# Attention, MoE and routed MoE on one core: inputs laid out for long rows, one VectorE step less per 64-bit piece, and a new order up to the first expert

## The chip, the cores and the metric

One core of one Trainium2 chip runs the whole program. The metric is device time in microseconds from launch to end. Three runs of the kernel before took 1063.85, 1066.41 and 1070.76 us; the median is 1066.41 us. In what follows PE is TensorE with its weight loads (PEld), DVE is VectorE, ACT is ScalarE, POOL is GpSimd, and SP is SyncE, whose queue issues nearly all DMAs. Every engine takes its own instructions strictly in the order in which they were written.

## The reference, cut to what matters

Three layers follow each other. Attention has 4 batches, 8 heads, 576 positions and head size 64, and sums two parts: a coarse attention over q, k and v averaged over groups of 4 positions, and a local one in which a position sees its 3 neighbours on each side. Then come a dense MoE layer with a squared relu, and a layer of 8 experts of which each token uses the two with the highest noisy gate value.

```
q_d, k_d, v_d = mean over groups of 4 positions
out = repeat(softmax(q_d k_d^T / 8) v_d, 4) + softmax(mask(q k^T / 8, |i-j| < 4)) v
x   = out as (2304, 512)
x   = relu(x @ w_in)^2 @ w_out                  # w_in (512, 2048), w_out (2048, 512)
y   = x @ w_gate + log1p(exp(x @ w_noise)) * noise;  top 2 of 8, softmax weights
out[token] += weight * (relu(x @ w1[e]) @ w2[e])  # for its two experts
```

w_in and w_out are float64 and reach the chip as 64-bit words, whose two halves the kernel joins to a float32 itself; everything else is float32.

## The kernel before, in words

Attention works on units: one batch, one pair of heads, one of two parts of the positions, so 32 units, numbered u = 8*batch + 4*part + pair. The dense layer works on 9 chunks of 256 tokens; a chunk's first product has 8 steps (M, 24 matmuls each), whose results are squared and split into a high and a low f16 half (r), and the second product has 8 steps (Y). All products are of split f16 operands, so three matmuls stand for one. The expert layer keeps an expert's weights split in the same way.

What sets the order is a table of names, ORDER, written out by hand up to the first expert's products: the program calls one small function per name, and each function's instructions go to the ends of their engines' queues. Names that the text uses:

- qk, vw, vg: DMA loads of q and k, of the windows of v for the local part, and of v in groups of 4.
- TQ, TK (L263 to L277): the transposes of q and k on PE, three blocks of 96 rows at a time into PSUM, and the copy of each half to qT or kT.
- GQ, GK (L279 to L289): sums of q and k over groups of 4, for batch 0 on POOL (three adds), for the others on DVE (one reduction).
- S, D (L307, L321): local and coarse scores. PT: transposes of the weights. PV, PW: products with v (L429 to L440). xa, xb: sums and f16 halves of the chunk's x.
- il, ib, ic, ij, is, in: one of 8 pieces of w_in: load; bits (two DVE steps, L528 and L529); scale (ACT, L533); join (DVE, L540); squares (ACT); column norms (PE). wS is the scale of all of w_in, whose maximum over partitions is made by POOL (L1003); wh, wl are the f16 halves (L1010, L1017).
- ol, oB, oc, oj, os, of, oh, oo: the same for 8 pieces of w_out, which hold a quarter of the columns and half of the rows each; oh and oo are the halves (L1073, L1078).
- yh, yl: steps of the second product of chunk 0, by quarters of the columns, as w_out arrives (L671). Y8 is the first full step of chunk 1 (L647).

A piece of 1 MB sits in a raw buffer (4 of them). For w_out the joined values go to one of four other places, and the raw buffer is free after the squares. q and k of batch 0 lie in the buffer of w_in's high half or in one buffer "qk"; a load into a buffer waits on SP's queue until its last reader is done, and all later loads wait behind it.

Two landmarks serve as stage bounds: M0, the first matmul of the dense layer (L608), and Y8.

Of the kernel before, what the change touches and what calls it, by code (L numbers as in the profile page):

```python
# [20 lines left out]
NP = H // 2  # L21
# [31 lines left out]
qk0 TQ0 TKa0 qk1 TQa1 GK0 GQ0 TK1 GQ1 il0 ib0 qk2 S0 ic0 D0 GK1 md0 S1 ed0 ml0 el0 il1 ij0 nl0 TQ2 is0 TKa2 qr0  # L53
nd0 GQ2 ib1 ic1 D1 md1 ed1 ml1 GK2 TR0 el1 nl1 nd1 PT0 S2 D2 GR0 md2 vg0 vm0 il2 ml2 el2 vs0 PT1 qk3 TQa3 ib2
ic2 TKa3 il3 ed2 S3 nl2 ij1 vw0 PV0 vg2 GQ3 GK3 D3 ib3 is1 vg1 nd2 ij2 ic3 ij3 vm1 vs1 vm2 ml3 vs2 el3 md3 il4
ib4 xa0 PT2 nl3 S4 D4 md4 vg3 vm3 Xa0 ml4 ed3 nd3 qr1 TRa1 S5 in1 is2 Xb0 in2 GR1 ic4 il5 ib5 vw1 PV1 el4 nl4
ij4 xb0 vs3 il6 is3 qr2 ic5 ij5 is4 ib6 ed4 xa1 PT3 D5 md5 il7 nd4 ic6 ij6 in4 ed5 ib7 TRa2 S6 xb1 ml5 is6 vw2
PV2 ic7 ij7 in3 in6 is5 xa2 in5 in0 el5 is7 PT4 ol0 oB0 vw3 in7 wS0 PV3 ol1 xb2 qr3 whd2 oc0 oj0 GR2 D6 oB1 xa3
wh0 wl0 wh7 TRa3 S7 wh3 xb3 wh1 os0 ol2 oB2 GR3 ol3 ol4 D7 wl1 wl2 oc1 oj1 wh5 M0 oB3 oc2 oj2 vw4 ra0 M1 M2 os1
ol5 oc3 wl7 vw5 os2 oj3 wl3 ra1 wl5 os3 of3 ol6 wh6 wl6 wh4 wl4 PW4 ob0 ra2 ol7 oh3 oh2 oB6 M3 M4 yh8 yh9 yh10  # L60
oo3 oB7 ra3 M5 oo2 oc6 oc7 oj7 oj6 ra4 yl8 yh11 os7 yl9 yl10 yl11 oB5 yh12 os6 of7 of1 nl5 ra5 M6 nd5 oh7 oo7
oh6 oh1 oc5 yl12 oh0 oo6 M7 oo1 oB4 PT5 oo0 yl24 yh24 yh13 oc4 yh25 yh0 oj4 yl25 qk4 TQa4 yh1 yl13 oj5 TKa4 yl26
xbd4 yl0 yh26 yl1 yh2 os4 md6 os5 yl2 SD0 pz0 ml6 yh27 yh3 of5 yl27 yl3 vg4 yh4 ra6 ed6 md7 vw6 yh28 el6 PW5
yh29 oh5 GK4 qk5 oh4 yl28 S8 TQa5 ed7 yl29 yh5 GQ4 D8 yh16 TKa5 pf5 yh17 nl6 nd6 yl4 PT6 ml7 el7 S9 vm4 pf3 xbd5
# [24 lines left out]
md30 D31 Y45 ra49 vw29 vw30 M50 el30 gf9 PT29 rd50 M51 ge9 gg9 ml31 ra51 PW29 xbd29 Y46 ed30 M52 nl30 nd30 el31
nl31 r52 Y47 ga10 md31 ed31 ga11 M53 r53 nd31 PT30 M54 PW30 gb10 xbd30 ra54 Y48 PT31 Y49 gb11 vw31 PW31 xbd31  # L90
gc10 gd10 gf10 M55 rd55 Y50 M56 AD0 gc11 gd11 Y51 M57 r56 r57 le0 pe0 pe1 ge10 gg10 pe2 pe3 pe4 gf11 Y52 M58 r58
Y53 M59 ge11 Y54 gg11 r59 M60 rd60 pe5 pe6 Y55 ga12 ga13 gb12 gb13 M61 r61 M62 pe7 Y56 gc12 gd12 Y57 gc13 pe8
ra62 gf12 Y58 gd13 gf13 Y59 M63 ge12 gg12 Y60 M64 Y61 pe9 r63 pe10 ge13 r64 pe11 gg13 M65 r65 pe12 pe13 Y62 M66
r66 Y63 ga14 ga15 gb14 gc14 M67 r67 M68 pe14 r68 Y64 Y65 gd14 Z0 M69 gb15 Z1 gf14 Y66 gc15 gd15 Z2 ge14 M70 gg14
ra69 M71 gf15 Z3 ge15 gg15 Y67 Y68 Y69 pe15 Z4 r70 Y70 Z5 pe16 r71 Y71 ga16 lr0 gb16 Z6 Z7 ga17 gb17 cm2 cm3 cm1
gc16 gd16 gf16 le1 cm0 cm6 cm7 cm5 ge16 gg16 gc17 cm4 pe17 gd17 pe18 pe19 pe20 gf17 pe21 pe22 pe23 cw0 ge17 gg17
cw1 pe24 pe25 pe26 lr1 cw2 cm9 cm11 pe27 cm10 cm8 pe28 cm15 cm14 lr2 cm13 cm12 pe29 pe30 cw4 pe31 pe32 cw3 pe33
le2
"""


@with_exitstack
def moe_kernel(ctx, tc, q, k, v, w_in, w_out, w_gate, w_noise, noise, w1, w2, out):
# [175 lines left out]
    def att_gi(b, hp, i, h=None):  # L279
# [6 lines left out]
        else:  # L286
            nc.gpsimd.tensor_tensor(dd, d4[:, :, 0], d4[:, :, 1], op=OP.add)
            for r in (2, 3):
                nc.gpsimd.tensor_tensor(dd, dd, d4[:, :, r], op=OP.add)  # L289
# [1011 lines left out]
```

## Time and profile before

| what | us |
|---|---|
| median of three runs | 1066.41 |
| span of the profiled execution | 1059.6 |
| median minus span | 6.8 |
| PE busy in the span | 945.8 (89%) |
| DVE busy | 623.7 (59%) |
| ACT busy | 485.3 (46%) |
| POOL busy | 161.9 (15%) |
| M0 starts (timeline) | 94.80 |
| Y8 starts (timeline) | 238.55 |

The page gives the span of the profiled execution, from its first to its last instruction, and not that execution's run time; what lies around the span is taken as the difference to the median. Busy shares over the whole span mix stages: PE has idle time until about 250 us and nearly none from there to 600 us. A DMA count on the page: 170115 packets, of them 129048 under 512 B.

### The profile page before, as it was taken

To read this page: it belongs to the slowest core of one execution; us is meant where nothing else is said; L and a number is where in the kernel's file an instruction comes from. 1 tells how busy PE (TensorE), PEld (TensorE's weight loads), DVE (VectorE), ACT (ScalarE), POOL (GpSimd) and SP (SyncE) were. 2 spreads that over 40 slices of the span, in tenths; PEclk is the share of its full clock that TensorE was granted. 3 is DMA by queue.
4 is the path that set the end of the run, shared out by engine and by line. 5 is a ranking of instruction groups with operands and counts; after the bars stand their busy time and mean duration, and the time that the engine had idled before them with its cause. 6 is when DMAs were issued, how large, how long until landed. Compare 5 with 4: busy or idle time off the path is not lost. (4 is left out here: it accounts for less than half of the span.)

```text
span 1059.6 us, 20935 instructions
## 1 busy us (share of the span) xinstructions
PE 945.8 (89%) x8351; PEld 636.9 (60%) x8351; DVE 623.7 (59%) x1883; ACT 485.3 (46%) x1065; POOL 161.9 (15%) x240
## 2 busy tenths in 40 slices
PE   3545788879999999999999999799999999999994
PEld 2334687655767677677766556465656565656562
DVE  4877896647877777777668674362525252525220
ACT  3656685544625464435445354372717171713110
POOL 5720020000101000100002212102020202021111
PEclk9999898989999999999999999899999999999997
DMA  6672376774223331211511265872737372730212
GB/s 191 187 233 78 121 198 200 215 235 87 82 57 86 74 83 32 61 51 37 191 41 51 68 203 118 234 212 39 217 40 218 40 215 42 217 40 11 39 17 36
DMA packets 170115, 121.69 MB, mean 115 GB/s; under 512 B 129048, under 2 KB 141848, under 8 KB 168984
## 3 DMA queue, kind: packets, MB, share of 16 engines
q1 hardware_dynamic: 161496, 100.52, 33.7%
q0 software_dynamic: 8512, 19.74, 9.3%
q8 instruction: 68, 1.11, 0.4%
q14 instruction: 39, 0.32, 0.1%
HBM read 70.28 MB, written 35.28 MB: 100 GB/s over the span
## 5 line engine op out<-in xcount | busy, mean ns | idle before, releaser
L608 PE MATMUL ph<-x,wih 128*128 128x256 f16 x1152 | 195.5, 275 | 0.0
L901 PEld LDWEIGHTS <-we 128*128 128x128 f16 x1536 | 151.8, 99 | 69.2 <-issue 15.6
L915 PE MATMUL po<-we,h 128*128 128x512 f16 (+1 forms) x840 | 182.4, 379 | 0.0
L608 PE MATMUL ph<-x,wil 128*128 128x256 f16 x576 | 158.4, 275 | 0.0
L901 PE MATMUL phc<-xT,we 128*128 128x384 f16 (+1 forms) x1152 | 154.4, 296 | 3.9 <-DVE h L904 3.9
L915 PEld LDWEIGHTS <-h 128*128 128x128 f16 (+1 forms) x840 | 87.5, 104 | 92.4
L647 PE MATMUL y<-wo,gh 128*128 128x512 f16 x448 | 134.7, 383 | 0.0
L903 ACT ACTIVATE h<-phc 128x384 f16<-128x384 f32 (+1 forms) x112 | 47.5, 430 | 177.1 <-PE phc L901 160.4
L608 PEld LDWEIGHTS <-wih 128*128 128x128 f16 x1152 | 111.4, 99 | 18.8 <-issue 1.0
L917 DVE TENSOR_SCALAR ob<-po,om 128x512 f32<-128x512 f32 (+1 forms) x35 | 26.3, 750 | 146.6 <-PE po L915 146.6
L918 POOL DMA_INDIRECT out_dram<-ob,tk x35 | 53.9, 1539 | 320.0 <-DVE ob L917 174.4
L808 POOL DMA_INDIRECT xs<-row,si x36 | 39.1, 1087 | 320.9 <-DVE xt L456 57.6
L647 PE MATMUL y<-wo,gl 128*128 128x512 f16 x224 | 85.4, 381 | 0.0
L904 DVE SCALAR_TENSOR_TENSOR h<-phc,h 128x384 f16<-128x384 f32 (+1 forms) x112 | 51.8, 476 | 52.0 <-ACT h L903 51.3
L647 PEld LDWEIGHTS <-gh 128*128 128x128 f16 x448 | 41.7, 98 | 42.3 <-issue 2.4
L608 PEld LDWEIGHTS <-wil 128*128 128x128 f16 x576 | 56.9, 99 | 7.1
L616 ACT ACTIVATE r<-ph 128x512 f32<-128x512 f32 x67 | 39.6, 591 | 26.4 <-PE ph L608 18.0
L620 ACT ACTIVATE g<-r 128x512 f32<-128x512 f32 x72 | 45.4, 630 | 11.9 <-DVE r L618 9.8
L630 DVE TENSOR_TENSOR gl<-g,gh 128x512 f16<-128x512 f32 x64 | 44.2, 691 | 9.2 <-ACT gh L629 8.0
L854 DVE SCALAR_TENSOR_TENSOR we<-w1raw,sce,we 128x1024 f16<-128x1024 f32 x32 | 40.5, 1278 | 3.9 <-ACT we L853 3.6
L321 PE MATMUL S<-kT,qT 64*64 64x144 f32 x192 | 22.3, 346 | 21.7 <-POOL qT L289 16.0
L854 DVE SCALAR_TENSOR_TENSOR we<-w2raw,sce,we 128x1024 f16<-128x1024 f32 x32 | 40.7, 1274 | 0.0
(347 smaller groups left out, 1477.3 us busy)
## 6 DMA issues: line engine op xcount, KB each, us to landing
w1raw<-in_moe_w_dram SPq DMA_DIRECT2D x8, 2048.0 KB
w2raw<-in_moe_w_dram SPq DMA_DIRECT2D x8, 2048.0 KB
xs<-zrow SPq DMA_DIRECT2D x8, 1290.0 KB
raw<-in_moe_w_out_dram SPq DMA_DIRECT2D x8, 1024.0 KB
raw<-in_moe_w_in_dram SPq DMA_DIRECT2D x7, 1024.0 KB
out_dram<-zrow SPq DMA_DIRECT2D x1, 4864.0 KB
qk<-in_k_dram SPq DMA_DIRECT2D x28, 144.0 KB
vw<-in_v_dram SPq DMA_DIRECT2D x94, 38.0 KB
```

The lines of the kernel that those rows point to most:

```text
L608: nc.tensor.matmul(ph[:, f], a[:, kk, fo], bb[:, kk], start=(n == 0), stop=(n == 11))
L616: nc.scalar.activation(r, ph, AF.Relu, scale=KAPPA)
L620: nc.scalar.activation(g, r, AF.Square)
L630: nc.vector.tensor_tensor(gl, g, gh, op=OP.subtract)
L647: nc.tensor.matmul(py[c, tt], a[:, o], bb[:, ft], start=(ft == 0 and n == 0), stop=(ft == 15 and n == 2))
L808: st = nc.gpsimd.indirect_dma_start(out=xs, out_offset=bass.IndirectOffsetOnAxis(ap=si[:, kk:kk + 1], axis=0), in_=roww, in_offset=None)
L854: nc.vector.scalar_tensor_tensor(wl[:, o], raws[i][:, o], ss[i], wh[:, o], op0=OP.mult, op1=OP.subtract)
L901: nc.tensor.matmul(ph[:, :n], a[:, fo], xT[:, bb], start=(i == 0), stop=(i == 11))
L903: nc.scalar.activation(hh[:, f], ph[:, :n], AF.Relu)
L904: nc.vector.scalar_tensor_tensor(hl[:, f], ph[:, :n], 0.0, hh[:, f], op0=OP.max, op1=OP.subtract)
L915: nc.tensor.matmul(po, a[:, f, jo], bb[:, do], start=(i == 0), stop=(i == 23))
L918: nc.gpsimd.indirect_dma_start(out=out, out_offset=bass.IndirectOffsetOnAxis(ap=tk[:m], axis=0), in_=ob[:m], in_offset=None, compute_op=OP ...
```

## The change

The host lays five inputs out anew (no arithmetic, only positions). q and k come already transposed, head pair by head pair, one row of 2 x 579 float32 per partition with three zeros behind each: one load of 593 KB takes the place of four to six of 72 to 144 KB, and TQ, TK and their copies are gone. v comes twice, once as windows with the 3 neighbours built in (38 rows of 2 or 3 KB, two copies per unit where there were four), once as groups of 4. w_out comes in the 8 pieces, with rows of 8 KB where they were 1 KB. The sums of q and k (G) are one DVE reduction per head pair, in batch 0 too.

Of a 64-bit piece the low word is now made by ACT (a new step, ia and oa, L495 of the new file), and DVE has one step (L499) where it had two. w_out's joined values stay in the raw buffer, which is free only after the low half oo. The loads of w_in's pieces 4 to 7 go to four places that are unused then. In chunks 1 to 5 the squared halves of the first three steps lie in three more buffers. The order table up to the first expert is new; r replaces its variants ra and rd (the f16 copy is on DVE in all 72 steps), and xb replaces xbd (the high half is on ACT for all 32 units).

```diff
@@ ORDER = """
-qk0 TQ0 TKa0 qk1 TQa1 GK0 GQ0 TK1 GQ1 il0 ib0 qk2 S0 ic0 D0 GK1 md0 S1 ed0 ml0 el0 il1 ij0 nl0 TQ2 is0 TKa2 qr0
+qk0 il0 ia0 vg1 G0 vg0 S0 vm1 ml0 el0 D0 md0 ed0 vm0 ib0 nl0 ic0 qk1 S1 nd0 vg3 vm3 qk2 G1 vs0 ml1 D1 PT0 S2 il1
...
-    def load_qk(b, hp, at_=None):
...
+    def load_qk(b, hp):
+        t = ap.tile([P, 2 * SD + 2 * (S + 3)], F32, tag="qkT", name=f"qkT{b}_{hp}", bufs=4)
+        nc.sync.dma_start(t[:, 2 * SD:], qk_in[b, hp])
+        qk[b, hp] = t
...
-            for j in range(2):
...
-                w = bass.AP(src.tensor, src.offset + (32 * (t0 + i0) - 3) * D, [[D, KW], [32 * D, i1 - i0], [1, D]])
-                nc.sync.dma_start(vt[h0:h0 + KW, i0:i1, j], w)
+            nc.sync.dma_start(vt[h0:h0 + KW, :n].rearrange("k t j d -> k (t j d)"),
+                              vwin[b, hp, :, t0:t0 + n].rearrange("k t c -> k (t c)"))
...
-    def att_ti(b, hp, i, evs=(EV, EV), gs=(0, 1)):
...
-                nc.tensor.transpose(pt[:, r * QT:(r + 1) * QT], src[:, 3 * g + r, :], idf[:QT, :QT])
-            evs[g](dst[:, 288 * g:288 * g + 288], pt[:, :288])
...
+    def att_g(b, hp, eng=None):
+        t = qk[b, hp]
+        dd = t[:, :2 * SD].rearrange("c (w g) -> c w g", w=2)
+        d4 = t[:, 2 * SD:].rearrange("c (w x) -> c w x", w=2)[:, :, :S].rearrange("c w (g r) -> c w g r", r=4)
+        if eng is None:
+            nc.vector.tensor_reduce(dd, d4, AX.X, OP.add)
...
+    xall = wp.tile([P, XB, 2, NP, CH], F16, name="xall")
+    xb = [xall[:, i] for i in range(XB)]
...
+        def low():
+            t_ = st["raw"][:, :, 0]
+            nc.scalar.activation(t_, t_.bitcast(U32), AF.Relu, scale=2.0 ** -29, bias=lob)
+
         def bits():
-            r16 = st["raw"].rearrange("p n w -> p (n w)").bitcast(U16).rearrange("p (n w) -> p n w", w=4)
-            nc.vector.tensor_scalar(r16[:, :, 0], r16[:, :, 1], 13, None, op0=OP.logical_shift_right)
-            nc.vector.tensor_scalar(r16[:, :, 1], r16[:, :, 3], 0x8000, None, op0=OP.bitwise_and)
+            t_, c_ = st["raw"][:, :, 0], st["raw"][:, :, 1]
+            nc.vector.scalar_tensor_tensor(t_, c_, -2 ** 31, t_, op0=OP.bitwise_and, op1=OP.bitwise_or)
...
+        return [load, low, bits, scale, join, st]
...
+        if 0 < c < 6 and fp < GX:
+            gh = ap.tile([P, 512], F16, tag="gh", name="gh", bufs=GX)
+            gl = ap.tile([P, 512], F16, tag="gl", name="gl", bufs=GX)
...
-        def place(h):
...
+            load, low, bits, conv, join, st_ = load_f(None, w_out[h])
...
+            w = (W["in"][1].rearrange("p k f -> p (k f)").bitcast(I32)[:, 2048 * n:2048 * n + 2048] if n < 2 else
+                 xall[:, 2 * n - 3:2 * n - 1].rearrange("p i a k c -> p (i a k c)").bitcast(I32))
...
+def _laid_out(inputs):
+    q, k, v = (np.asarray(inputs[n]) for n in "qkv")
+    qk = np.zeros((B, NP, 2, D, 2, S + 3), q.dtype)
+    for i, a in enumerate((q, k)):
+        qk[..., i, :S] = a.reshape(B, NP, 2, S, D).transpose(0, 1, 2, 4, 3)
...
```

How the change moves instructions, at three places. On PE just ahead of M0 the order before was this (S is a tile of scores, kT and qT transposed k and q, wih and x the dense layer's operands):

```order
L321 MATMUL S<-kT_2_313,qT_2_312 64x144 x4
L276 MATMUL ptq<-idf,qk_3_431 128x96 x3
L307 MATMUL S<-kT_3_437,qT_3_436 32x38 x20
L321 MATMUL S<-kT_3_437,qT_3_436 64x144 x4
L608 LDWEIGHTS wih
L608 MATMUL ph<-x_158,wih 128x256
```
and in the change:

```order
L966 LDWEIGHTS xall
L966 MATMUL pn<-onesb,xall 128x1
L263 MATMUL S<-qkT_0_685 32x38 x16
L577 LDWEIGHTS wih
L577 MATMUL ph<-xall,wih 128x256
```
The transpose and the coarse scores of two units (L321) stood ahead of M0; in the change only column norms and local scores (L263) that need no sum of q or k.

On DVE, pieces of w_in being joined (raw and wil hold raw words, vi the joined values). Before:

```order
L528 TENSOR_SCALAR raw<-raw 128x1024
L529 TENSOR_SCALAR raw<-raw 128x1024
L358 TENSOR_REDUCE rs<-pm_143 128x5
L540 SCALAR_TENSOR_TENSOR vi<-raw 128x1024
L479 SCALAR_TENSOR_TENSOR x_158<-xt,sx_645,x_158 128x256
L540 SCALAR_TENSOR_TENSOR vi<-raw 128x1024
L528 TENSOR_SCALAR wil<-wil 128x1024
L529 TENSOR_SCALAR wil<-wil 128x1024
L456 TENSOR_TENSOR xt<-px,od 128x256
```
and in the change:

```order
L508 SCALAR_TENSOR_TENSOR vi<-raw 128x1024
L499 SCALAR_TENSOR_TENSOR raw<-raw 128x1024
L436 SCALAR_TENSOR_TENSOR xall<-xt,sx_456,xall 128x256
L314 TENSOR_REDUCE rs<-pm_143 128x5
L499 SCALAR_TENSOR_TENSOR wil<-wil 128x1024
L319 TENSOR_SCALAR rs<-rs 128x5
L320 RECIPROCAL rs<-rs 128x5
L508 SCALAR_TENSOR_TENSOR vi<-raw 128x1024
L413 TENSOR_TENSOR xt<-px,od 128x256
```
Two steps per piece and one join (L528, L529, L540) have become one step and one join (L499, L508), with the attention's small steps between them as before.

On SP, the loads of w_in from the fifth on, before:

```order
L524 DMA raw<-in_moe_w_in_dram 128x2048
L194 DMA wil<-in_v_dram 72x4x256
L227 DMA wih<-in_q_dram 96x3x64 x2
L524 DMA raw<-in_moe_w_in_dram 128x2048
L259 DMA vw_152<-in_v_dram 38x4x64 x4
L524 DMA wil<-in_moe_w_in_dram 128x2048
L227 DMA wih<-in_q_dram 96x3x64 x2
L524 DMA raw<-in_moe_w_in_dram 128x2048
```
and in the change, from the second on (four loads of q and k with two of v are partly ahead of it):

```order
L491 DMA raw<-in_moe_w_in_dram 128x2048
L190 DMA wih<-in_vgrp_dram 72x1024
L223 DMA qkT_3_337<-in_qk_dram 128x1158
L491 DMA raw<-in_moe_w_in_dram 128x2048
L230 DMA vw_151<-in_vwin_dram 38x512 x2
L491 DMA raw<-in_moe_w_in_dram 128x2048
L491 DMA wil<-in_moe_w_in_dram 128x2048 x2
L230 DMA vw_152<-in_vwin_dram 38x512 x2
L491 DMA xall<-in_moe_w_in_dram 128x2048
L230 DMA vw_151<-in_vwin_dram 38x512 x2
L491 DMA xall<-in_moe_w_in_dram 128x2048
```
The loads of a second half of q into buffers still read by transposes (L227) stood between w_in's; now q and k of batch 0 have four buffers of their own and stand ahead, and only window loads (L230) are between.

## Rows read from the trace of the kernel before

**Rows 1.** Windows to M0, to Y8, beyond; per engine busy us (instructions).
```profile
core 0: us, PE busy (x) PEld busy (x) DVE busy (x) ACT busy (x) POOL busy (x), PEclk, DMA share, GB/s
0.00:94.80 94.80, 39.12 (x568) 28.41 (x568) 61.14 (x104) 46.59 (x100) 45.70 (x89) 1.00 0.61 178
94.80:238.50 143.70, 116.09 (x1611) 100.23 (x1609) 105.96 (x238) 90.27 (x216) 7.46 (x27) 0.89 0.65 189
238.50:600.00 361.50, 360.98 (x3573) 248.25 (x3570) 272.79 (x1119) 171.19 (x440) 37.38 (x73) 1.00 0.26 71
```

**Rows 2.** PE's waits before M0: us in total, times, longest.
```profile
PE S L321 <- POOL qT L289: 16.0, 4, 10.0
PE ptp L384 <- POOL pm L366: 11.6, 2, 11.0
```

**Rows 3.** Timeline, four engines: start us, us, engine, work [idle before <-releaser].
```profile
12.80 1.31 DVE L528 TENSOR_SCALAR raw<-raw 128x1024 uint16<-128x1024 uint16 x1
...
65.50 0.43 POOL L366 TENSOR_TENSOR pm<-pm,rs 128x152 f32<-128x152 f32 x1 [9.68 <-issue]
...
81.01 0.38 POOL L1003 PARTITION_ALL_REDUCE n2w<-cm__866  x1 [8.05 <-issue]
...
86.66 1.27 DVE L1017 SCALAR_TENSOR_TENSOR wil<-vi,s_in,wih 128x1024 f16<-128x1024 f32 x1
...
88.71 0.30 POOL L287 TENSOR_TENSOR qT<-qT 128x72 f32<-128x72 f32 x1 [7.33 <-issue]
...
89.96 1.23 PE L321 MATMUL S<-kT,qT 64*64 64x144 f32 x8 [10.01 <-POOL qT L289]
...
94.80 0.61 PE L608 MATMUL ph<-x,wih 128*128 128x256 f16 x2
```

**Rows 4.** The same windows, the transposes alone (L276).
```profile
94.80:238.50 143.70, 8.82 (x72) 6.97 (x72) 0.89 0.65 189
238.50:600.00 361.50, 7.98 (x72) 7.14 (x72) 1.00 0.26 71
```

**Rows 5.** Groups on DVE, 0 to 262 us: xcount, busy us, mean ns.
```profile
L529 DVE TENSOR_SCALAR raw<-raw 128x1024 uint16<-128x1024 uint16 x15 | 21.9, 1459 | 0.5
L528 DVE TENSOR_SCALAR raw<-raw 128x1024 uint16<-128x1024 uint16 x15 | 20.5, 1364 | 3.7 <-DMA raw<-in_moe_w_out_dram 3.7
...
L540 DVE SCALAR_TENSOR_TENSOR vi<-raw 128x1024 int32<-128x1024 int32 x7 | 9.3, 1336 | 0.0
...
L285 DVE TENSOR_REDUCE qT<-qT 128x144 f32<-128x576 f32 x6 | 4.4, 743 | 0.0
```

**Rows 6.** Groups on ACT, 0 to 262 us.
```profile
L533 ACT ACTIVATE raw<-raw 128x1024 f32<-128x1024 f32 x15 | 17.3, 1151 | 19.6 <-DVE raw L529 19.5
...
L277 ACT COPY qT<-ptq 128x288 f32<-128x288 f32 x20 | 7.4, 395 | 19.2 <-PE ptq L276 19.1
```

**Rows 7.** Timeline of SP's DMA issues.
```profile
38.06 12.71 SPq L259 DMA_DIRECT2D vw<-in_v_dram  x4
50.88 0.99 SPq L524 DMA_DIRECT2D wil<-in_moe_w_in_dram  x1
...
71.96 24.25 SPq L522 DMA_DIRECT2D raw<-in_moe_w_out_dram  x3
...
216.06 17.60 SPq L259 DMA_DIRECT2D vw<-in_v_dram  x4
```

**Rows 8.** PE's waits from M0 to Y8.
```profile
PE px L437 <- DMA vw<-in_v_dram: 10.9, 6, 5.4
PE y L671 <- DVE wo L1078: 5.1, 1, 5.1
PE pfr L487 <- ACT raw L1063: 3.3, 1, 3.3
PE ptq L276 <- ACT qT L277: 2.8, 2, 1.7
PE ptq L276 <- DMA qk<-in_q_dram: 2.5, 2, 1.5
```

More of the change, by code (lines that the diff above doesn't have):

```diff
@@ L99, with moe_kernel @@
+lr0 gc16 gb17 cm6 gd16 gc17 le1 gf16 gd17 cm7 pe17 ge16 pe18 gf17 gg16 cm0 cm3 cm1 pe19 pe20 ge17 pe21 gg17 cm2
+cm4 pe22 cm5 pe23 pe24 cw1 pe25 pe26 pe27 cw0 lr1 pe28 cw2 cm15 pe29 cm10 cm9 pe30 cm11 cm8 pe31 cm14 pe32 cm13
+cm12 pe33 lr2 le2 cw4 cw3
 """
 @with_exitstack
-def moe_kernel(ctx, tc, q, k, v, w_in, w_out, w_gate, w_noise, noise, w1, w2, out):
+def moe_kernel(ctx, tc, qk_in, vwin, vgrp, w_in, w_out, w_gate, w_noise, noise, w1, w2, out):
     nc = tc.nc
@@ L413, in moe_kernel @@
     xc = {}
-    xb = [wp.tile([P, 2, NP, CH], F16, name=f"x{i}") for i in range(XB)]
+    xall = wp.tile([P, XB, 2, NP, CH], F16, name="xall")
+    xb = [xall[:, i] for i in range(XB)]
     def att_pv(*u):
@@ L533, in scale, with join @@
             nc.scalar.activation(c_, c_, AF.Copy, scale=2.0 ** -112)
[L535 removed]
+        def join():
             c_, t_ = st["raw"][:, :, 1], st["raw"][:, :, 0]
[L537 to L542 removed]
+            st["v"] = dst if dst is not None else c_.bitcast(F32)
+            nc.vector.scalar_tensor_tensor(st["v"].bitcast(I32), c_, 3, t_, op0=OP.logical_shift_left,
+                                           op1=OP.bitwise_or)
+        return [load, low, bits, scale, join, st]
     def prep_gate():
@@ L1079, in lo @@
                                         op0=OP.mult, op1=OP.subtract)
-            return [load, lambda: st[h][1](), lambda: st[h][2](), join, sq, scale, hi, lo]
+            return [load, low, bits, conv, join, sq, scale, hi, lo]
         return begin, [piece(h) for h in range(8)]
@@ L1272, in moe_kernel @@
                 nc.vector.tensor_scalar(cur, cur, float(P), None, op0=OP.add)
-_INS = ["q", "k", "v", "moe_w_in", "moe_w_out", "moe2_w_gate", "moe2_w_noise", "moe2_noise", "moe2_w1", "moe2_w2"]
+_INS = ["moe_w_in", "moe_w_out", "moe2_w_gate", "moe2_w_noise", "moe2_noise", "moe2_w1", "moe2_w2"]
 _OUTS = [((NTOK + TRASH, DM), "float32")]
+def _laid_out(inputs):
+    import numpy as np
+    q, k, v = (np.asarray(inputs[n]) for n in "qkv")
+    qk = np.zeros((B, NP, 2, D, 2, S + 3), q.dtype)
+    for i, a in enumerate((q, k)):
+        qk[..., i, :S] = a.reshape(B, NP, 2, S, D).transpose(0, 1, 2, 4, 3)
+    qk = qk.reshape(B, NP, P, 2 * (S + 3))
+    vp = np.zeros((B, H, S + KW, D), v.dtype)
+    vp[:, :, 3:S + 3] = v
+    vwin = np.empty((B, NP, KW, S // 32, 2, D), v.dtype)
+    for t in range(S // 32):
+        vwin[:, :, :, t] = vp[:, :, 32 * t:32 * t + KW].reshape(B, NP, 2, KW, D).transpose(0, 1, 3, 2, 4)
+    vgrp = v.reshape(B, NP, 2, 2, SD // 2, 4, D).transpose(0, 4, 1, 2, 3, 5, 6).reshape(B, SD // 2, NP, 16 * D)
+    out = {"qk": qk, "vwin": vwin.reshape(B, NP, KW, S // 32, 2 * D), "vgrp": vgrp}
+    for n in _INS:
+        a = np.asarray(inputs[n])
+        if n == "moe_w_out":
+            a = a.reshape(2, 8, P, 4, P).transpose(3, 0, 2, 1, 4).reshape(8, P, 8 * P)
+        out[n] = a.view(np.int64) if a.dtype == np.float64 else a
+    return {n: np.ascontiguousarray(a) for n, a in out.items()}
 def kernel(**inputs):
@@ L1287 @@
     arrays, args = {}, []
-    for name in _INS:
-        a = _np.ascontiguousarray(inputs[name])
-        if a.dtype == _np.float64:
-            a = a.view(_np.int64)
+    for name, a in _laid_out(inputs).items():
         arrays[f"in_{name}_dram"] = a
```

243 lines of the change are left out of this document (82 added, 161 removed).

## The prediction

> **What bounds the kernel now.** I read the windows first, cut at two landmarks that both kernels pass: M0, the first matmul of the dense layer, and Y8, the first full step of the second product of chunk 1 [rows 1]. The reader is to see three stages. Up to M0 (94.8 us) no engine is full: DVE is busy 61.1 us, ACT 46.6, PE 39.1. From M0 to Y8 (143.7 us) PE is busy 116.1 us and waits 27.6. From Y8 to 600 us PE is busy 360.98 of 361.50 us: there, a microsecond of PE work is a microsecond of the kernel, and what other engines do costs nothing while they keep up (DVE 272.8 of 361.5). Then the waits: ahead of M0, PE waits 16.0 us for POOL's sums of q and 11.6 us for POOL's normalising [rows 2]; from M0 to Y8 it waits most for the windows of v, 10.9 us [rows 8]. Last the timeline, which tells why POOL is late [rows 3]: around the two maxima over partitions, POOL stands idle 7.33 to 9.68 us with no releaser in the profile, before the maximum at 81.01 and after it at 65.50 and 88.71. I take it that POOL changes its code there, since all three gaps are next to that one kind of instruction.
>
> **M0.** M0's own operands are there when the slice of the low half of w_in ends, 86.66 + 1.27 = 87.9 us. PE is not: in its order the scores of two units stand ahead of M0, and the first of these waits until 89.96 for a sum that POOL makes after its gap. PE comes to M0 at 94.80, 6.9 us late [rows 3]. In the change PE has only column norms and local scores ahead of M0, none of which reads POOL's work behind the second maximum, and the sums are on DVE. So 6.9 us go.
>
> How much earlier are M0's operands? They come out of the eight joined pieces of w_in, through DVE and ACT.
> - DVE, per piece: two steps of 1.36 and 1.46 us become one. The trace has no such step with two inputs and bit operations on 1024 words but the join, 1.34 us, of the same shape [rows 5]; I take that. It saves 1.49 us a piece, 15 us for the ten pieces begun before M0 (8 of w_in, 2 of w_out). Added are five sums for q and k together, at 2 x 0.743 = 1.49 us each, 7.4 us. Net DVE loses 7.5 of 61.1 us.
> - ACT: the new step on the low words, 1024 words at a stride of two, as the scale step is: 1.15 us [rows 6]. Ten of these stand ahead of the first slice of w_in's high half, 11.5 us. Thirteen copies of transposed q and k at 0.40 us go, 5.2 us [rows 6]. Net ACT gains 6.3 us and comes to 52.9. A piece now passes five times between DVE, ACT and PE instead of four.
> - SP: loads of w_in are no longer held behind loads of q that wait for transposes, and the window copies between them are half as many. The four copies at 38.06 took 12.71 us of SP's queue, and the piece behind them went out at 50.88 [rows 7]. The data will be there before DVE wants them.
>
> DVE thus lets go of 7.5 us and ACT takes on 6.3, with both near 53 us of work. Bounds for M0: not before 12.8 us (the first piece on DVE [rows 3]) plus ACT's 52.9 plus the last slice on its way, 4 us, so about 70; and at worst, if the extra hop eats every freed microsecond and M0 queues elsewhere, the 94.8 of now. Between these I put the operands at 84, 4 us earlier than now, half of DVE's 7.5, since the two engines wait for each other in turn. **M0 at 84: -10.8 us** (70 to 95: -25 to 0). PE's transposes before M0 lie in its idle time and count nothing.
>
> **M0 to Y8.** Between the two landmarks both orders hold 18 steps M and 64 quarter steps yh and yl. The change does three local scores and one value product less here and does them later, at the same price, so they cancel. Off PE go 72 transposes, 8.8 us [rows 4]. Of PE's waits, the 2.8 and 2.5 us for transposes go. Of the 10.9 us for windows of v [rows 8] I take half: two copies per unit instead of four (one set of four held SP for 17.60 us [rows 7]), but the data still queue behind larger loads. The bounds are none and all of it. The waits for w_out (5.1 and 3.3 us) stay, and here something is added: w_out's second half is loaded into raw buffers that come free only when the low half of the first is done, one after the other. I add 3 us (0 to 8). Waits: 27.6 - 5.3 - 5.4 + 3 = 20. DVE (106 us now) takes over twelve f16 copies and loses six times 1.49 us and five single sums (eleven become three double ones); ACT loses most copies of q and k and gains six steps of 1.15 us; neither comes near PE's sum. **-16.5 us** (-9 to -25).
>
> A rule speaks against my half. The Trainium skill, DMA: Bandwidth & Descriptors (in "Why a DMA increments its semaphore by 16 and not by 1"), says that such a copy uses the largest number of engines, 16 at most, that divides its slowest dimension on both sides; for 38 rows that would be 2 engines, before and after. No row here shows which engines a copy used. By this the landing would not get earlier, the 10.9 us would stay, and the sum would be 5.4 us higher.
>
> **After Y8.** 72 transposes, 7.98 us of PE's work [rows 4], where PE has no idle time: **-8.0 us**. The copies behind them, the f16 copies (now on DVE in all steps) and the x halves (now on ACT) move between engines that are busy 75% and 47% here [rows 1]: nothing. If DVE came to its limit, each of the 17 copies that it takes over would cost its own length; by the nearest row, a copy of 288 columns at 0.40 us [rows 6], that is 7 us. From the first expert on nothing but the order of the last steps changes; I take nothing, within 4 us to either side.
>
> **Sum.** -10.8 - 16.5 - 8.0 = -35.3 us against the profiled span of 1059.6, so 1024.3; the median of the runs lies 6.8 above that span, and the sum goes against it: **1031 us**, 3.3% faster.
>
> **Rivals.**
> - *ACT takes DVE's place.* The hop through ACT eats what DVE frees, M0 stays at 94, the waits to Y8 stay, and the transposes alone (8.8 + 8.0 us) are gained: 1066.4 - 16.8 = 1050, with a spread of 1043 to 1058. For: ACT's sum grows by 6 us and becomes as large as DVE's. Against: the 6.9 us behind POOL go in any case. Chance 0.17.
> - *Windows stay late*, by the rule above as a mechanism of this kernel: the copies of v keep their landing time and PE its 10.9 us: 1036. For: the longest wait, 5.4 us, falls where bulk writes fill the DMA engines. Chance 0.14; it lies inside the forecast's range.
> - *More than I allow.* Both front engines overlap well, M0 at 72 (12 us more), and waits to Y8 fall to 10 (10 us more): 1009, spread 1000 to 1017. For: the granted clock is 0.89 from M0 to Y8 and 1.00 beyond, where PE does not wait [rows 1]; fewer waits may raise it. Chance 0.14.
> - *Slower: w_out's ring.* The second half of w_out waits on SP's queue for the first half's low halves. Meanwhile PE has chunk 0's eight of the 18 steps M and half of the 64 quarter steps to do, by their share some 45% of 116 us, so from M0 to about 135 us. If each pair of buffers came free as slowly as SP's queue moved at 71.96, where three w_out loads took 24.25 us [rows 7], two such rounds are 48.5 us: 1031 + 48.5 = 1079. It decides once the third quarter's high half is later than about 170 us, when PE's idle time has eaten the 35 us. Against: from its landing a piece needs five steps of 1.1 to 1.4 us. Chance 0.05.
> - *Given back.* PE reaches the experts 35 us earlier and waits there for rows or weights: 1061. Against: their loads are issued in the same order and move forward with PE. Chance 0.03.
>
> **Numbers.** The forecast has the rest, 0.47, with a range of its own of 1020 to 1042. The range of all, 1004 to 1053, leaves out the slower case, the case given back, a third of ACT's case (0.06) and a quarter of the good one (0.03): 0.17. A measurement of this kernel tells 1% from no change, 11 us. Faster by more than that means under 1055.7: 0.47 + 0.14 + 0.14 + 0.14 of ACT's case = 0.89; within 1%: 0.06; slower: 0.05.
>
> **What will show it.** M0 between 78 and 90 us with PE's last wait before it not on POOL. From M0 to Y8 PE's busy time down by 7 to 11 us and its waits near 20, those for windows of v between 2 and 9. DVE's one step at 1.2 to 1.4 us, ACT's at 1.1 to 1.2. From Y8 on PE full as before and the stretch from Y8 to the first expert's products 6 to 10 us shorter. I am wrong in the front if M0 is after 92; wrong on w_out if PE waits over 10 us for a half of it; wrong on the whole if the gain up to Y8 is there and the end is not.

## The result, and the profile after

The changed kernel takes 1016.05 us (median of 4 runs, 1012.51 to 1017.29) beside 1065.13 us of the kernel before in the same comparison: a ratio of **0.954** (95% interval 0.950 to 0.958). In a second comparison it was 0.9534 (0.9497 to 0.9571). That is 49 us, where 35 were forecast. The profiled execution took 1015.63 us, its span is 1013.6 us, 46.0 less than before.

The windows of the changed kernel, cut at M0, Y8, the first product of the first expert, the first product of the third expert (E2), and the last product of the experts' first layer. They answer to [rows 1].

```profile
core 0: us, PE busy (x) PEld busy (x) DVE busy (x) ACT busy (x) POOL busy (x), PEclk, DMA share, GB/s
0.00:73.70 73.70, 27.23 (x543) 20.42 (x543) 55.87 (x105) 52.36 (x101) 19.35 (x45) 1.00 0.72 250
73.70:184.30 110.60, 101.56 (x1413) 87.44 (x1414) 93.19 (x212) 86.81 (x191) 8.57 (x13) 0.95 0.65 224
184.30:555.10 370.80, 367.12 (x3644) 248.83 (x3643) 274.93 (x1106) 172.05 (x450) 37.65 (x66) 1.00 0.29 75
555.10:671.80 116.70, 110.78 (x671) 66.50 (x670) 57.76 (x184) 57.66 (x104) 18.15 (x16) 0.94 0.65 173
671.80:969.70 297.90, 288.21 (x1773) 178.89 (x1772) 116.21 (x222) 115.61 (x199) 40.02 (x27) 0.98 0.46 98
```

The same stretches of the kernel before, from Y8 on.

```profile
238.50:611.10 372.60, 370.73 (x3617) 252.56 (x3614) 277.59 (x1125) 174.38 (x445) 40.82 (x77) 1.00 0.27 72
611.10:729.30 118.20, 109.31 (x671) 65.71 (x671) 59.08 (x189) 58.59 (x105) 20.29 (x16) 0.96 0.65 173
729.30:1017.60 288.30, 284.36 (x1772) 177.51 (x1771) 115.74 (x222) 115.13 (x199) 39.95 (x26) 1.00 0.43 101
```

Stage by stage, before to after: up to M0 94.8 to 73.7 (-21.1); M0 to Y8 143.7 to 110.6 (-33.1), PE's busy time 116.1 to 101.6 and its waits 27.6 to 9.0; Y8 to the first expert 372.6 (238.5 to 611.1) to 370.8 (-1.8); the experts, to the end of the span, 448.5 to 458.5 (**+10.0**), of which 9.6 lie between E2 and the last product of the first layer. The sum is -46.0.

PE's five longest waits ahead of M0 (pm and pd are the local and the coarse weights); this answers to [rows 2].

```profile
PE S L277 <- DVE pm L286: 14.7, 3, 10.9
PE S L263 <- ACT pd L309: 8.3, 3, 6.3
PE S L263 <- DMA qkT<-in_qk_dram: 5.3, 1, 5.3
PE ph L577 <- ACT wih L982: 3.8, 1, 3.8
PE ptp L340 <- POOL pm L322: 3.1, 1, 3.1
```

Of the 27.6 us on POOL's sums of q and its normalising [rows 2] 3.1 are left. The reader is to see that PE now hangs on DVE and ACT, the two engines that make w_in. The timeline up to M0 (POOL, ACT, PE), which answers to [rows 3]:

```profile
31.68 0.72 POOL L206 TENSOR_TENSOR vd<-wih 72x256 f32<-72x256 f32 x1
38.46 0.38 POOL L213 PARTITION_ALL_REDUCE xm<-xm  x1 [6.06 <-issue]
...
69.32 0.38 POOL L975 PARTITION_ALL_REDUCE n2w<-cm__788  x1 [15.49 <-DVE cm__788 L973]
...
70.43 3.24 ACT L982 ACTIVATE wih<-vi,s_in 128x1024 f16<-128x1024 f32 x3
...
73.72 0.61 PE L577 MATMUL ph<-xall,wih 128*128 128x256 f16 x2 [3.79 <-ACT wih L982]
```

The sum of q and k on DVE, and the new steps of a piece on DVE and on ACT (xcount | busy, mean ns); they answer to [rows 5, 6]:

```profile
L240 DVE TENSOR_REDUCE qkT<-qkT 128x288 f32<-128x1152 f32 x16 | 21.5, 1341 | 1.1 <-DMA qkT<-in_qk_dram 1.1
L499 DVE SCALAR_TENSOR_TENSOR raw<-raw 128x1024 int32<-128x1024 int32 x12 | 14.6, 1218 | 0.2 <-ACT raw L495 0.2
L495 ACT ACTIVATE raw<-raw,lob 128x1024 int32<-128x1024 uint32 x12 | 14.7, 1233 | 0.0
```

PE's waits from M0 to Y8, which answer to [rows 8]: nothing is left of the 10.9 us for windows of v. The first row is the wait that ends at M0, shown above; it belongs to the stage before.

```profile
PE ph L577 <- ACT wih L982: 3.8, 1, 3.8
PE ph L577 <- DVE wil L989: 2.6, 1, 2.6
PE pfr L444 <- ACT raw L1011: 2.1, 2, 1.5
PE y L643 <- DVE gh L599: 2.0, 1, 2.0
PE y L643 <- ACT wo L1020: 1.5, 1, 1.5
```

### The profile page after: what moved, and what is told of

It is laid out like the page before. It is cut to its first block, busy times and chain, and to the rows that moved or that the text cites. A ratio compares the mean times of both kernels' runs of the same rounds, so it can differ in the third digit from the quotient of the medians.

```text
span 1013.6 us, 20138 instructions
## 1 busy us (share of the span) xinstructions
PE 921.0 (91%) x8159; PEld 614.6 (61%) x8159; DVE 602.1 (59%) x1833; ACT 484.9 (48%) x1043; POOL 131.4 (13%) x171
## 5 line engine op out<-in xcount | busy, mean ns | idle before, releaser
L577 PE MATMUL ph<-xall,wih 128*128 128x256 f16 x1152 | 197.6, 278 | 3.9 <-ACT wih L982 3.8
L873 PE MATMUL phc<-xT,we 128*128 128x384 f16 (+1 forms) x1152 | 158.2, 300 | 9.7 <-DVE h L876 9.7
L577 PE MATMUL ph<-xall,wil 128*128 128x256 f16 x576 | 159.6, 277 | 2.7 <-DVE wil L989 2.6
L780 POOL DMA_INDIRECT xs<-row,si x36 | 36.9, 1026 | 338.5 <-issue 133.5
L577 PEld LDWEIGHTS <-wil 128*128 128x128 f16 x576 | 57.3, 100 | 10.9 <-DVE wil L989 3.1
L585 ACT ACTIVATE r<-ph 128x512 f32<-128x512 f32 x72 | 42.3, 587 | 19.8 <-PE ph L577 19.0
L825 ACT ACTIVATE we<-w1raw,sce 128x1024 f16<-128x1024 f32 x32 | 35.2, 1139 | 18.5 <-DVE sce L158 15.2
L599 DVE CAST gh<-g 128x512 f16<-128x512 f32 x64 | 27.1, 423 | 26.2 <-ACT g L589 25.3
```

The source lines that it names most:

```text
L577: nc.tensor.matmul(ph[:, f], a[:, kk, fo], bb[:, kk], start=(n == 0), stop=(n == 11))
L585: nc.scalar.activation(r, ph, AF.Relu, scale=KAPPA)
L780: st = nc.gpsimd.indirect_dma_start(out=xs, out_offset=bass.IndirectOffsetOnAxis(ap=si[:, kk:kk + 1], axis=0), in_=roww, in_offset=None)
L873: nc.tensor.matmul(ph[:, :n], a[:, fo], xT[:, bb], start=(i == 0), stop=(i == 11))
```

## Experiments

Three questions: which part gives the front its 21 us, which one took the waits up to Y8 away, and what gives 10 us back at the experts. "The changed kernel" of each expectation is the one of the second comparison: 1009.35 us and 0.9534, from which losses and gains are counted. All ratios are to the kernel before on the same chip, whose median is 1058 to 1060 us there, so 0.01 is 10.6 us.

**The changed kernel again.**

> The changed kernel as it is, so that the others of this call have it beside them on the same chip. Expected: M0 at 73 to 75 us, the first expert at 554 to 557, and a ratio to the kernel before of 0.95 to 0.958, as in the comparison that gave 0.954. If the second expert starts by 672 us and the stretch from there to the last first-layer matmul is again 294 to 298 us (288.3 before the change), the give-back belongs to the kernel; if it is 288 to 290, it was that one execution's.

M0 at 73.5, Y8 at 185.0, the first expert at 551.9, E2 at 667.0, and from E2 to the last first-layer product 296.5 us. The first expert came 2 us earlier than I expected; the give-back is the kernel's own.

**The old two steps on DVE back.**

```diff
 def low():
-    nc.scalar.activation(t_, t_.bitcast(U32), AF.Relu, scale=2.0 ** -29, bias=lob)
+    pass
...
 def bits():
-    nc.vector.scalar_tensor_tensor(t_, c_, -2 ** 31, t_, op0=OP.bitwise_and, op1=OP.bitwise_or)
+    nc.vector.tensor_scalar(r16[:, :, 0], r16[:, :, 1], 13, None, op0=OP.logical_shift_right)
+    nc.vector.tensor_scalar(r16[:, :, 1], r16[:, :, 3], 0x8000, None, op0=OP.bitwise_and)
```

> The changed kernel with the old bit work: two DVE steps per 64-bit piece, no step on ACT. My theory (DVE's work sets M0): in the trace of the changed kernel DVE is busy 9.1 to 9.9 of each 10 us from 40 us to M0 at 73.7, and two steps (1.36 + 1.46 us) in place of one (1.22 us) are 1.6 us more a piece, 16 us for the ten pieces ahead of M0 and 9.6 us for the six of w_out behind it, where DVE is busy over 95% until 110 us. M0 comes 8 to 16 us later and the kernel is 10 to 20 us slower. Rival (the new order and the loads give the front its gain, and ACT, full from 60 to 110 us, is as much a bound as DVE): the 1.24 us a piece that ACT is spared pay for DVE's 1.6, M0 moves by less than 4 us, and the time by less than 5 us, down as well as up.

1032.02 us, ratio 0.9757 (0.9737 to 0.9776): 24 us lost, a little over my range. M0 came at 86.0 (+12.3) and M0 to Y8 took 118.5 us (+7.9), in which PE's wait for a raw buffer's square on ACT rose from 2.1 to 9.7 us. Ahead of M0 DVE was busy 10.9 us more (66.8 to 55.9; I had expected 16), ACT 9.8 us less. The rival falls: ACT's relief, 1.23 us a piece, pays for nothing.

**The sums on POOL again.** The order's G0 to G3 became Gp0 to Gp3, which the program has for this.

> The changed kernel with the column sums of the first four units' q and k on POOL again (three additions for each pair in place of one DVE step of 1.34 us). DVE is spared 5.4 us ahead of M0. My theory (sums on POOL hold PE, as the 16.0 us of PE's waits for them before the change show): the far scores wait for POOL, which is held behind its own other work, and M0 is 4 to 10 us later, the kernel 4 to 12 us slower than the changed one. Rival (DVE's work alone counts): M0 comes 2 to 5 us earlier and the kernel is as much faster.

1019.5 us, ratio 0.9625 (0.9605 to 0.9644): 10 us lost, all of it ahead of M0 (84.2). PE's longest wait and POOL's timeline in this kernel:

```profile
PE S L277 <- POOL qkT L244: 25.3, 4, 13.6
```

```profile
40.05 2.81 POOL L244 TENSOR_TENSOR qkT<-qkT 128x288 f32<-128x288 f32 x2
50.04 0.38 POOL L213 PARTITION_ALL_REDUCE xm<-xm  x1 [7.17 <-issue]
57.18 1.27 POOL L205 TENSOR_TENSOR wih<-wih 72x512 f32<-72x512 f32 x1 [6.76 <-ACT raw L503]
```

The gap ahead of POOL's maximum is no new one (7.17 us, and 6.06 in the changed kernel). What moved is the work in front of it: with the sums it ends at 42.86 us, without them at 32.40 (31.68 + 0.72), and the maximum comes at 50.04 in place of 38.46, 11.6 us later, as M0 comes 10.5 us later.

**PE's transposes alone put back.**

```diff
 def att_g(b, hp, eng=None):
     t = qk[b, hp]
+    for g in range(4):
+        pt = psT.tile([P, 512], F32, tag="tp", name="dum")
+        for r in range(3):
+            o = 2 * SD + P * (3 * (g % 3) + r)
+            nc.tensor.transpose(pt[:, r * QT:(r + 1) * QT], t[:QT, o:o + P], idf[:QT, :QT])
```

> The changed kernel with 12 more PE transposes of 96 rows for each of the 16 units of q and k, ahead of the unit's column sums in the program; nobody reads what they write, so only PE's work of the transposes that the change removed is put back, not the copies behind them. My theory (PE's work counts where PE is full, which is now from 120 us on): of the 192, the 48 of batch 0 lie in PE's idle time ahead of M0; 144 at 0.245 us are 35 us if all ran at the price of the full stretch as single instructions, but in groups of three the rows of before give 0.11 to 0.12 us each (8.82 us for 72, 7.98 us for 72): 16 us slower, spread 13 to 18. Rival (what lies ahead of Y8 is hidden in PE's waits): only the second 72 count, 8 us slower, spread 6 to 10.

1027.91 us, ratio 0.9723 (0.9697 to 0.9748): 20 us lost, above both theories' spreads, nearer to mine. By the instruction counts 61 of them stand ahead of M0, 36 up to Y8 and 96 behind. M0 is 3.5 us later although PE waits there, M0 to Y8 takes 3.7 us more, and Y8 to the first expert 379.5 us in place of 366.9 to 370.8. The transposes ahead of M0 are not free.

**Short rows for the windows of v, and four copies of long rows.**

```diff
-nc.sync.dma_start(vt[h0:h0 + KW, :n].rearrange("k t j d -> k (t j d)"), vwin[b, hp, :, t0:t0 + n]...)
+for j in range(2):                                       # short rows
+    nc.sync.dma_start(vt[h0:h0 + KW, :n, j], vwin[b, hp, :, t0:t0 + n, 64 * j:64 * j + 64])
+for i0, i1 in ((0, n // 2), (n // 2, n)):                # the other kernel: four copies, long rows
+    nc.sync.dma_start(vt[h0:h0 + KW, i0:i1].rearrange("k t j d -> k (t j d)"), vwin[b, hp, :, t0 + i0:t0 + i1]...)
```

> The changed kernel with the windows of v loaded in four copies of 256-byte rows in place of two copies of rows of 2 to 3 KB; the data and their place in the order are the same. My theory (the layout of v took the waits for windows away: 13.1 us in the whole kernel before, 0.9 us after): PE waits 5 to 11 us for windows again, and the kernel is 4 to 11 us slower. Rival (the order took them away, since the windows are asked for earlier against their use): waits for windows stay under 2 us and the time within 2 us.

> The changed kernel with each of the two copies of a unit's windows of v split by windows into two: four copies per unit, as in the kernel before, but of long rows (1 to 1.5 KB). With four copies of 256-byte rows the kernel lost some 24 us, and SP's queue stood 14.38 us on the first four where two long-row copies took 2.18. Theory A (the many short rows hold SP's queue): four long-row copies cost SP little, each about 0.3 to 1 us, and the time stays within 5 us of the changed kernel. Theory B (the number of copies holds it): SP stands on them about as long as in the 256-byte kernel, and 15 to 25 us are lost again.

Short rows: 1033.89 us, ratio 0.9775 (0.9755 to 0.9795), **25 us** lost, far over what I expected, yet PE's own wait for windows is only 5.5 us. Four long copies: 1011.97 us, 0.9552 (0.9519 to 0.9584), 2 us, less than the two intervals can tell apart. What the short rows do to SP's queue is seen in the timelines of the changed kernel, the one with short rows and the one with four long copies (start us, us, copies at the end):

```profile
10.80 2.18 SPq L230 DMA_DIRECT2D vw<-in_vwin_dram  x2
...
19.72 1.82 SPq L230 DMA_DIRECT2D vw<-in_vwin_dram  x2
```

```profile
10.91 14.38 SPq L231 DMA_DIRECT2D vw<-in_vwin_dram  x4
25.33 1.11 SPq L491 DMA_DIRECT2D raw<-in_moe_w_in_dram  x1
...
27.49 10.34 SPq L231 DMA_DIRECT2D vw<-in_vwin_dram  x4
```

```profile
11.02 5.58 SPq L231 DMA_DIRECT2D vw<-in_vwin_dram  x4
...
24.97 5.94 SPq L231 DMA_DIRECT2D vw<-in_vwin_dram  x4
```

The same bytes hold the queue 14.38 us in short rows and 2.18 in long ones, and the loads behind stand there. Theory A holds: the rows, and much less the number of copies (though four long ones take 5.58 us, more than I expected). Ahead of M0 the hold costs little: M0 is at 76.2 us with short rows and at 76.3 with four long copies, against 73.5. The 25 us come behind M0. M0 to Y8 took 120.1 us (+8.6 against the 111.5 of the changed kernel in the second comparison) with PE waiting 6.0 us for DVE's normalising and 4.8 for a square on ACT, and Y8 to the first expert 379.6 (+12.7 against 366.9), with PE's 5.5 us for windows. The wait of 6.0 us can be followed back to the queue (SP, ACT, DVE, PE; vg is v in groups of 4, jv what ACT makes of it):

```profile
140.40 16.77 SPq L231 DMA_DIRECT2D vw<-in_vwin_dram  x8
157.28 1.18 SPq L190 DMA_DIRECT2D vg<-in_vgrp_dram  x1
...
162.21 0.63 ACT L199 ACTIVATE jv<-vg 72x512 bf16<-72x512 f32 x1 [6.61 <-DMA vg<-in_vgrp_dram]
...
163.71 0.69 DVE L205 TENSOR_TENSOR vg<-vg 72x512 f32<-72x512 f32 x1 [7.32 <-ACT jv L199]
...
165.57 0.67 PE L340 MATMUL ptp<-idf,pm 128*102 128x128 f32 x2 [6.04 <-DVE pm L322]
```

and the same two loads in the changed kernel:

```profile
135.46 8.99 SPq L230 DMA_DIRECT2D vw<-in_vwin_dram  x4
144.62 0.30 SPq L190 DMA_DIRECT2D vg<-in_vgrp_dram  x1
```

The load of vg goes out behind the windows of two units, at 157.28 in place of 144.62; ACT waits for it, DVE for ACT, and PE for the normalising that stands behind it on DVE. The other waits were not followed back like this. The Trainium skill (Perfetto Trace Analysis, "What 'DMA-bound' means") reads a queue that is solid with DMA work as the making of descriptors, for which large descriptors matter; these rows agree.

**Two parts alone in the kernel before.** The windows of v from the laid-out array, and the one step on DVE with its step on ACT.

> The kernel before with one part of the change alone: the windows of v from the laid-out array in two copies of long rows; order, transposes and the two DVE steps as before. My theory (SP's queue and the windows limit the kernel before, too): the four copies at 38 us no longer hold SP for 12.71 us and the ones at 216 us not for 17.60, PE's 13.1 us for windows fall below 3, and the kernel is 10 to 20 us faster than before. Rival (before the change the front hangs on POOL's sums and on DVE, and the freed time turns into waits there): 0 to 6 us faster.

> The kernel before with one part of the change alone: per 64-bit piece one step on ACT and one on DVE (1.23 and 1.22 us in the changed kernel) in the place of two on DVE (1.36 and 1.46). Order, transposes and loads are as before. Putting the two steps back in the changed kernel made M0 12.3 us later and lost 23 us in all. My theory (DVE is the bound of the front only where loads and sums don't hold it; in the old order PE comes to M0 6.9 us late behind POOL): M0 moves by less than 5 us, M0 to Y8 by less than 5 us, and the time by less than 6 us to either side. Rival (DVE's work is what sets the front in either order): 16 us of DVE go from the front, M0 comes 8 to 14 us earlier, and the kernel is 10 to 20 us faster.

The windows alone: 1056.78 us, 0.9978 (0.9961 to 0.9996), 2 us gained. The step alone: 1059.65 us, 0.9998 (0.9982 to 1.0014), nothing. M0 stood at 94.0 and 95.0; the step freed 14.7 us of DVE's work ahead of it (61.1 to 46.4) for nothing, as I expected. For the windows my theory missed in two points. The whole gain is not 10 to 20 us: M0 to Y8 fell from 143.7 to 131.1 us, but the stretch from E2 grew from 288.3 to 297.5 and took most of it back, so the small gain is not the rival's either, which looked for new waits at the front. And PE's waits for windows did not fall below 3 us:

```profile
PE px L427 <- DMA vw<-in_vwin_dram: 9.6, 3, 4.0
```

Before they were 13.1 us. So the layout alone does not take them away; in the changed kernel, with the layout and the new order, 0.9 us are left, and with the new order and short rows 5.5. Of the 12.4 us that PE idled less from M0 to Y8, 5.4 are waits for windows, 5.1 waits of the transposes of q and k, and 3.2 the wait for a half of w_out: all loads on SP's queue or steps behind them. PE's two longest waits ahead of M0 with the step alone:

```profile
PE S L321 <- POOL qT L289: 17.7, 4, 12.6
PE ptp L384 <- POOL pm L366: 16.4, 3, 11.8
```

DVE is freed and PE goes on waiting for POOL.

**More buffers for the experts' small tiles.** The edit is one number, 3 or 6 in place of 2, in the changed kernel, and 6 in the kernel before.

```diff
-nb = 1 if pool is sp else 2
+nb = 1 if pool is sp else 6
```

> The changed kernel with three buffers in place of two for the small tiles of an expert's rows (slots, weights, token numbers). In the traces the stretch from the second expert's products on PE to the end is 11.5 us longer after the change than before it, and the one difference that I find is DVE's copy of the token numbers, which waits for the scatter that still reads the buffer: 35.0 us in four waits after, 29.3 before; behind it on DVE stand the steps that PE waits for (9.7 us after, 3.9 before). My theory (this wait gives back part of the gain): with a third buffer DVE does not wait there, PE's 9.7 us go, with them most of the lower clock that follows each stop (0.93 and 0.97 in two of the 50 us stretches), and the kernel is 8 to 14 us faster than the changed one. Rival (the scatters themselves, 5.7 us apart, hold the output tiles next): the wait moves to the output tiles' buffers, and the time changes by less than 3 us.

> The changed kernel with six buffers for the small tiles of an expert's rows, one for each expert that takes its rows there. With three, DVE's copy of the token numbers still waited three times (23.8 us) for the scatters, since the order on DVE then has the copy for an expert further ahead right behind the output steps whose scatters read that buffer; with six no buffer is used twice and the copy has nothing to wait for. My theory (PE's 9.7 us at the first layer of the experts come from that wait): no wait of DVE for a scatter, PE's wait for DVE there under 3 us, and 6 to 12 us faster than the changed kernel. Rival (PE would next wait for weights or output tiles): under 3 us.

> The kernel before with six buffers for the small tiles of an expert's rows, and nothing else. With six, the changed kernel's stretch from the third expert's first product on to its last fell from 296.5 to 283.9 us. My theory (the copy of token numbers waits for scatters in the kernel before, too, but its scatters land sooner there): the stretch falls from 288.3 to 284, PE's idle time there from 3.9 to 0, and the kernel is 3 to 6 us faster than before. Against this kernel the changed one with six buffers should then show what the change gives ahead of the experts alone, some 54 to 57 us. Rival (before the change the wait costs as much as after it, and the one profiled execution was a good one): 9 to 13 us faster.

With three: 1007.59 us, 0.9526 (0.9506 to 0.9547), no difference that can be told; the copy on DVE waited three times instead of four (23.8 us). The stretch from E2 did fall, to 290.6 us, but that from Y8 to the first expert was 370.4, and it varies between 366.9 and 370.8 from one execution of the changed kernel to the other. My theory as I put it for three buffers missed. With six: **997.32 us**, 0.9407 (0.9376 to 0.9438), 12.0 us faster than the changed kernel beside it, and the fastest kernel here. In the kernel before, six gave 1056.31 us, 0.9966 (0.9944 to 0.9989), 4 us, as I expected. The wait in the changed kernel, on DVE and then on PE (tk are the token numbers, ob the rows that a scatter adds to the output, phc an expert's first product and h its low half):

```profile
790.45 0.17 DVE L862 CAST tk<-mt 128x5 int32<-128x5 f32 x1 [10.79 <-DMA out_dram<-ob,tk]
790.53 1.48 DVE L876 SCALAR_TENSOR_TENSOR h<-phc,h 128x384 f16<-128x384 f32 x3
```

```profile
791.13 17.94 PE L873 MATMUL phc<-xT,we 128*128 128x384 f16 x132 [4.46 <-DVE h L876]
```

DVE's waits for scatters in all, in the kernel before and in the changed one; with six buffers there is no such row in either.

```profile
DVE tk L890 <- DMA out_dram<-ob,tk: 29.3, 4, 7.9
```

```profile
DVE tk L862 <- DMA out_dram<-ob,tk: 35.0, 4, 10.8
```

And the stretch from E2 with six buffers, in the changed kernel and in the kernel before, where PE does not wait at all and the granted clock stays at 1.00:

```profile
668.00:951.90 283.90, 283.90 (x1773) 177.34 (x1772) 115.46 (x206) 115.56 (x199) 39.95 (x26) 1.00 0.47 102
```

```profile
730.10:1013.90 283.80, 283.80 (x1772) 176.99 (x1771) 115.38 (x206) 115.50 (x199) 39.93 (x26) 1.00 0.43 102
```

The two are alike, where with two buffers the changed kernel was 9.6 us longer here: the copy's wait is what gave the 10 us back.

**An array that nobody reads.**

> The kernel before with one more input array of 11.2 MB (zeros, of the size of the laid-out windows of v) that no instruction reads; all instructions are the same. In every kernel with changed inputs the rows' transposing load of one or two experts takes 12.4 to 13.6 us, where all four of the kernel before take 9.9 to 10.3, the scatters next to it land later, and the stretch from the third expert's first product to its last takes 293 to 299 us in place of 288.3; this holds for the kernel before with the windows of v alone, too, whose gain of 12.6 us up to Y8 is given back there. Theory (where the arrays lie in memory sets it): 293 to 299 us here too, and 4 to 9 us slower than before. Rival (the instant at which loads and scatters meet sets it): 287 to 290 us, and the time within 2 us.

(The array has 5.6 MB; the 11.2 in the expectation is my slip.) 1065.38 us, 1.0048 (1.0028 to 1.0067): 5 us slower with the same instructions. The stretch from E2 took 291.4 us, and one of its four transposing loads 12.30 us where the kernel before has 9.9 to 10.3. In the kernel with six buffers, with the arrays of the changed one, none took more than 11.76, so the "every kernel" of the expectation doesn't hold. That is between the two theories: where the arrays lie does matter, but this array doesn't make the whole 297.9 of the changed kernel. Whether the changed kernel's later scatters come from its new arrays or from the instant at which loads and scatters meet stays open.

## Why the prediction was right, and where its terms were not

The time lies in the range of 1004 to 1053, and the side was right. The forecast's own range of 1020 to 1042 misses it by 4 us. The forecast of 1031 is 15 us too high. Of these, 10.7 are in the stages (46.0 us against 35.3), and 4.4 in the 6.8 us added for what lies around the span: measured are 2.45 (1016.05 less 1013.6), and wherever the run time and the span of one execution are both on record they are 1.7 to 2.1 us apart. The 6.8 set the median of three runs against the span of another execution, and so took the spread between runs into the sum. What happened is the rival "more than I allow" almost to the letter (M0 at 72 and waits of 10 us up to Y8; the trace has 73.7 and 9.0), and then 10 us given back at the experts, a place that I had named in another rival, with the wrong mechanism. That the time lies in the range is partly luck: up to Y8 the stages gained 54.2 us where 27.3 were forecast, and behind Y8 they lost 8.2 where a gain of 8.0 was forecast. Of the signs that I listed, M0's last wait and DVE's step came, and ACT's nearly (1.23 us); M0's time, PE's busy time and waits up to Y8, the waits for windows and the stretch behind Y8 all lay outside what I had stated.

- **M0, -10.8 forecast, -21.1 measured.** The sums were right within 2.3 us: DVE 53.6 forecast (61.1 less 7.5) and 55.9 measured, ACT 52.9 and 52.4. The reading of POOL was right: PE's last wait before M0 is for ACT's slice of w_in, and with the sums on POOL again M0 is 10.5 us later. The step that failed is "Between these I put the operands at 84, 4 us earlier than now, half of DVE's 7.5". I let the idle time of the engines stand. DVE's, ahead of M0, fell from 33.7 to 17.8 us; from 40 us on it was busy 9.1 to 9.9 of each 10 us. What went were waits behind other engines; for loads of w_in DVE waits in neither kernel there (ACT, which takes a piece first after the change, waits 8.2 us for the first). Its two waits in the kernel before that are gone (S are scores, x a half of the chunk's x on ACT):

```profile
DVE nb L342 <- PE S L321: 8.0, 2, 4.5
DVE x L479 <- ACT x L476: 5.8, 1, 5.8
```

PE's scores stood behind POOL's sums [rows 2]. So POOL held PE, and PE held DVE, which makes w_in; I had priced the first only. In the changed kernel DVE waits 0.2 us for scores, and with the sums on POOL again 8.0 us, with 32.0 us idle in all. With DVE that full, each microsecond of its work is one of M0, as the two steps show: 10.9 us of work more, 12.3 us of M0. My own lower bound of about 70 us, from ACT's sum, was nearer than the middle that I took.
- **M0 to Y8, -16.5 forecast, -33.1 measured.** Of the 16.6 us between, 11 are waits (20 forecast, 9.0 measured): I took half of the 10.9 us for windows and had the price of the rest in the wrong place. I priced the layout of v by PE's waits for windows; in the kernel with short rows those waits are 5.5 us of 25, and the rest is with what stands behind the copies on SP's queue. The rival "windows stay late" did not come: the copies still have 38 rows, and PE's waits for them went from 13.1 us in the whole kernel to 0.9. But it is not refuted for the layout alone, which left 9.6. No row shows which engines the copies used, nor when they landed. The 3 us that I added for w_out's ring didn't come (3.3 to 2.1 us for its square), and the slower rival with it. Another 4.4 us are no gain: the scores and value products that the change puts behind Y8 cancel in the kernel, but not in this stage, where I let them cancel (their groups behind Y8 come to 53.9 us of PE's time, before to 49.5).
- **After Y8, -8.0 forecast, -1.8 measured** (-5.7 in the second execution). The 7.98 us of transposes went, the 4.4 us of moved work came, and PE waited 3.7 us instead of 1.9.
- **The experts, 0 within 4 forecast, +10.0 measured.** "I take nothing" was wrong. DVE's copy of the token numbers waits there for scatters in both kernels, and I had not looked for it since PE's wait was 3.9 us in all. It was close to the edge: 5.7 us more of waiting on DVE made 5.8 us more of PE's between E2 and the end of the first layer (3.9 to 9.7); the other 3.9 us of the 9.6 are matmuls that took longer, at a mean granted clock of 0.98 against 1.00. Why the scatters land later is open. With six buffers in both kernels the change is worth 0.9407 / 0.9966 = 0.944, some 59 us, and in the profiled executions 57.2 us lie ahead of the experts (609.3 to 552.1).
- **The parts don't add.** Taken back singly from the changed kernel they cost 24 (step), 25 (rows of v), 20 (transposes) and 10 us (sums), 79 in all, more than the 49 that it gained. Alone in the kernel before, the step gave 0: PE's waits for POOL hid it. The windows gave 13.4 us up to Y8 there, where I had allowed 5.4 for them, and lost all but 2 again at the experts. A sum of terms from the profile of before, each priced with the other waits in place, was therefore too low here. The new order, the layout of w_out and the added buffers for squared halves were not tested by themselves; what each of them gave is not known.

## What to carry to other kernels

Where several engines and queues take turns to be late, a change that takes away all of them at once is worth more than its parts by the profile of before: price the new state as a whole, by the busiest engine's sum and the idle time that is left to it, not by halving. Here the bound from ACT's sum was 70 us for M0, the halved gain gave 84, and 73.7 were measured. Look at how long a copy holds the queue that issues it before looking at who waits for its data. When PE comes sooner to a later stage, look there for an engine that stands in order behind a landing (here a copy behind scatters); a few more buffers for some bytes were worth 12 us.

## What the runs showed of the hardware

- The windows of each of the first four units (38 partitions), in the order of the changed kernel, held SP's queue for 6.21 to 14.38 us as four copies of 256-byte rows, and for 0.56 to 2.18 us as two copies of long rows. In the old order a unit's two long-row copies held it for 0.62 to 5.80 us ahead of M0.
- In the changed kernel DVE's step of 1.22 us (L499) took 3.57 us at 48.25, while POOL ran six of its own in a row (starting from 48.14 to 50.69), and POOL's step of 0.44 us (L322) took 1.27 at 27.85, beside that step of DVE.
- An input array that no instruction reads made the same instructions 0.48% slower (0.28 to 0.67%).
